# Banded attention and feed-forward on one core: exclusive or in the weight words, a range check by a second read, g folded into w1, seven products from chunk 3, and a new order

## The chip, the cores and the metric

One core of a Trainium2 chip runs the whole program. TensorE (PE; PEld is its weight load), VectorE (DVE), ScalarE (ACT) and GpSimd (POOL) each take their instructions in order; SyncE (SP) issues nearly all DMAs, also in order. The metric is the device time of one execution in microseconds, the median of the runs.

## The reference

```python
scores = scale * np.matmul(q, k.transpose(0, 1, 3, 2))          # (4, 8, 768, 64) each
keep = is_global | is_local                                     # 8 first keys, and the 96 before
scores = np.where(keep, scores + bias, -1e9)
a = np.exp(scores - scores.max(-1)); a = a / (a.sum(-1) + 1e-9)
x = (a @ v) as (4, 768, 512)
xn = (x - mu) / np.sqrt(var + 1e-06) * g_ln
out = x + np.maximum(xn @ w_ch1, 0.0) @ w_ch2                   # (512, 2048) and (2048, 512)
```

[...]

## The kernel before, in words

**Tiles.** The 3072 tokens are 24 tiles of 128 (`t`), two to a chunk (`c`, 12 of them). Tiles 0 to 3 are the first tiles of the four batches; they are "short", with one key block, and are computed in 32-bit floats. All others take two key blocks, with every operand as a high and a low half-precision part, so that a product becomes three.

**Tasks.** All work is given as tasks to a planner (`Plan`), with an engine (or several, with a cost each), a cost, the tasks that it waits for, a rank, and the buffers that it takes. `Plan.order` is a list scheduler on these numbers; what it puts out is the order in which the instructions are written, and each engine then keeps that order. Where PE would idle in the first 90 us it writes products of no use (`blank`). Every instruction is issued through one helper, so all rows have that one line (L204 before, L248 after), and are told apart by their tiles.

**Attention of tile t.** Loads `Lk`, `Lq`, `Lv`; in short tiles `tk`, `tq` (a transpose on PE) and `km`, `qm` (the copy out). `S` scores on PE (tile `s`), `R` mask and row minimum on DVE (`T<-s,mask`), `E` exponentials on ACT, `tp` the transpose of the weights (in long tiles `ph`, `pl` split them and `pt` is a DMA transpose), `P` weights by values (`pv`). Then the normalisation: `X`, `B`, `A` on DVE (`x<-pv,r`, `st<-x`, `mv<-st`), `W` a power on POOL (`rs<-rs,half`), `C` centring on DVE (`xs`), then `xh` and `xl`, the halves of the transposed x (`xT`; for short tiles through a PE transpose `tx`). A long tile with i > 1 also needs 16 key and value rows copied into its neighbour's tile (`gk`, `gv`).

**Weight piece n of 16** (0 to 7 of w1, 8 to 15 of w2): `wb` loads 1 MB, `wr` (ACT) rounds the low word down to three bits, `ws` (DVE) puts the sign into the low word, `wz` (ACT) takes the size of the high word and accumulates a maximum for the range check, `ww` (DVE, `st<-st`, int32) shifts and joins the words, `wu` makes the high half and `wl` the low half.

**Feed-forward.** `F{c}_{f}` is a first-layer step (24 products of 128x256); it needs both tiles' `xT` and weight pieces f//4*2 and the next one. In chunks 0 to 3 (`EVEN = 4`) `hh` and `hl` split its result and `G` is the plain second layer, 96 products of 128x512 a chunk. From chunk 4 on the second layer is done by a seven-product scheme on halves: `hr`, `hm` and `hh`, `hl` make seven mixed operands (`R`, `uh`, `ul`), `N{c}_{n}` are the products (21 of 128x256 for each pair of f, 168 a chunk), `D` combines the sums, and `ya`, `yh`, `yl` make the mixed weights beforehand. `O` stores a tile.

**The end.** `M` (ACT) sums squares of the weights, `K0` judges ranges, `K1` is a small product (`pf`) after `F11_14` that sums over partitions, `K2` writes a flag and `K3` reads it on every engine; it chooses whether a general fallback runs behind.

Of the kernel before, what the change touches and what calls it, by code (L numbers as in the profile page):

```python
# [54 lines left out]
SIDE = (-1.1, 1.1)  # L55
# [24 lines left out]
EVEN = 4  # L80
EARLY = 150.0
LEAD = 11
VRANK = 6.0
VLATE = 0.0
WEIGH = (-0.8, 0.2)
FAVOR = {"ACT": SIDE[0], "POOL": SIDE[1]}
LATER = {"ACT": WEIGH[0], "POOL": WEIGH[1]}
EITHER = {"ACT": 0.62, "DVE": 0.7}
BLANK = 0.22


class Plan:

    def __init__(self, lag=0.12):
        self.tasks, self.room, self.lag, self.blank, self.until = {}, {}, lag, None, 0.0

    def task(self, key, engine, cost, fn, after=(), rank=0.0, take=None, dma=0.0, slack=0.0, port=False):
        assert key not in self.tasks, key
        costs = dict(engine) if isinstance(engine, dict) else {engine: cost}
        self.tasks[key] = costs, fn, [a for a in after if a is not None], rank, take or {}, dma, slack, isinstance(engine, dict), port  # L100

    def order(self):
# [25 lines left out]
        while len(self.times) < len(tasks):  # L128
# [38 lines left out]
            end = t + cost  # L167
# [22 lines left out]
def banded(ctx, tc, q, k, v, n_global, n_local, g_ln, w1, w2, out, flag):  # L190
# [58 lines left out]
    fill = const.tile([P, 1], F32, name="fill")  # L249
# [3 lines left out]
    def starts():  # L253
# [23 lines left out]
    def asked():  # L277
        made["asked"] = counts(const, act, n_global, n_local)
# [49 lines left out]
    task("gb", "SP", 0.6, lambda: load.dma_start(out=gb, in_=g_ln.partition_broadcast(P)), rank=9, dma=0.7)
# [7 lines left out]
    def weight(n):  # L336
# [20 lines left out]
        def signs():  # L357
            vec.tensor_scalar(out=halves[n][:, :, 1], in0=halves[n][:, :, 3], scalar1=0x8000, scalar2=None, op0=ALU.bitwise_and)

        def sizes():  # L360
            hi = staged[n][1]
            act.activation(out=hi.bitcast(F32), in_=hi.bitcast(F32), func=AF.Abs, scale=2.0 ** -111, accum_out=big[:, n:n + 1])

        def whole():
            lo, hi, _, _ = staged[n]
            vec.scalar_tensor_tensor(out=hi, in0=hi, scalar=3, in1=lo, op0=ALU.logical_shift_left, op1=ALU.bitwise_or)

        def upper(engine):
# [12 lines left out]
        task(f"wb{n}", "SP", 0.6, bring, before, rank=rank - 12, take={} if n in homes else {"st": [f"wl{n}"]}, dma=3.0)  # L381
        task(f"wr{n}", "ACT", 1.24, below, [f"wb{n}", "starts"], rank=rank)
        task(f"ws{n}", "DVE", 0.7, signs, [f"wr{n}"], rank=rank, port=True)
        task(f"wz{n}", "ACT", 1.2, sizes, [f"ws{n}"], rank=rank)
        task(f"ww{n}", "DVE", 1.22, whole, [f"wz{n}"], rank=rank, port=True)
        task(f"wu{n}", {"ACT": 1.17, "POOL": 1.95, "DVE": 0.75}, 0, upper, [f"ww{n}"] + (["wl1"] if n == 8 else []) + (["wl3"] if n in (8, 9, 10, 11) else []) + (["wl7", "wl8"] if n >= 12 else []), rank=rank, port=True)
        task(f"wl{n}", {"POOL": 2.2, "DVE": 1.24}, 0, lower, [f"wu{n}"], rank=rank, port=True)
# [16 lines left out]
    def sums_of_weights(j):  # L404
# [26 lines left out]
        cost = {"DVE": 0.68, "POOL": 1.2}  # L431
        last = ["room"] + [f"wl{8 + 2 * j + a}" for a in range(2)]

        def chain_of(n, first, ats, rank, final, last):
# [4 lines left out]
            task(f"yh{n}_{j}", {"ACT": 0.6, "DVE": 0.45}, 0, lambda engine: high(engine, n), last, rank=rank, take={"h": ["never"]} if n == 4 else {}, port=True)  # L439
# [4 lines left out]
        last = chain_of(3, (0, 1), (((0, 1, 1), ALU.subtract), ((1, 0, 1), ALU.add), ((1, 1, 1), ALU.subtract)), rank, 4, last)  # L444
# [3 lines left out]
        chain_of(1, (0, 1), (((0, 0, 0), ALU.subtract), ((1, 0, 1), ALU.add), ((1, 0, 0), ALU.subtract)), rank, 1, last + [f"G{CT * EVEN - CT}_{4 * j + 2}"])  # L448
# [38 lines left out]
    def quick(t, rank):  # L487
# [8 lines left out]
        def loads(name, src, r):  # L496
            task(f"L{name}{t}", "SP", 0.57, lambda: fetch(raw, (name, t), src, name, b, i), rank=rank + r - 12 * (t == 0), take={"ld": [f"P{t}_1" if name == "v" else f"t{name}{t}"]}, dma=1.47)
# [5 lines left out]
        def both(name, make, scale):  # L503
# [8 lines left out]
            task(f"t{name}{t}", "PE", 0.7, flip, [f"L{name}{t}", "ident"], rank=rank, take={bank: [f"{name}m{t}"]}, slack=0.5 * (t > 1))  # L512
# [7 lines left out]
    def keys(t, b, i, rank):  # L520
# [21 lines left out]
        task(f"kh{name}", {"ACT": 0.64, "DVE": 0.5}, 0, high, [f"Lk{name}"], rank=rank, take={"ld": [f"kt{name}"]}, port=True)  # L542
        task(f"kl{name}", {"POOL": 1.22, "DVE": 0.7}, 0, low, [f"kh{name}"], rank=rank, port=True)
# [833 lines left out]
```

## Time and profile before

| what | value |
|---|---|
| time, median of 3 runs | 608.65 us (607.88 to 608.71) |
| profiled execution, first to last instruction | 605.5 us |
| PE, DVE, ACT, POOL busy | 591.0, 514.9, 408.6, 160.8 us |
| granted PE clock over the span | 0.999 |
| DMA moved | 88.33 MB |

The profiled execution shows its span only; the median of the runs is 3.15 us above it, which is what lies before the first and after the last instruction, and the two are compared with that constant between them. Busy shares are averages over a start, in which PE waits for inputs, a long middle, and a tail of a few microseconds.

### The profile page before, as it was taken

Reading aid. Unit: us, or ns where it says so; the run is one execution under the profiler, and the core shown is the slowest. Engines: PE = TensorE matmul, PEld = TensorE weight load, DVE = VectorE, ACT = ScalarE, POOL = GpSimd, SP = SyncE. Lnnn points to the kernel's source line nnn. Section 1 sums busy time; section 2 is a strip of 40 time slices with the busy share of each in tenths; the row PEclk is TensorE's granted clock in tenths of the full one; section 3 lists DMA queues with packets and bytes.
Section 4 is the critical chain, followed back from the end, with each engine's and each line's share of the span. In section 5 each row is a group of like instructions: output and inputs, shape, how many; then the busy total and the mean of one; then the engine's idle time right before and its main releaser. Section 6 shows DMA issues by size and latency. Waiting matters only on the chain.

```text
span 605.5 us, 15320 instructions
## 1 busy us (share of the span) xinstructions
PE 591.0 (98%) x5929; PEld 489.7 (81%) x5929; DVE 514.9 (85%) x1244; ACT 408.6 (67%) x1004; POOL 160.8 (27%) x128
## 2 busy tenths in 40 slices
PE   8989999999999999999999999999999999999996
PEld 4767896556965985789999999999999999988885
DVE  5999999999999989899789999898898788484654
ACT  5988897965677865787765766889856756333330
POOL 2310121306463228242042122152232031040100
PEclk9999999999999999999999999999999999999999
DMA  8993999976879985977748676868865423110001
GB/s 217 321 312 102 238 221 193 244 183 132 221 165 183 183 191 130 202 158 108 156 125 141 139 157 123 162 137 160 154 141 123 105 55 88 36 40 16 35 2 37
DMA packets 247307, 88.33 MB, mean 146 GB/s; under 512 B 237376, under 2 KB 237376, under 8 KB 247232
## 3 DMA queue, kind: packets, MB, share of 16 engines
q1 hardware_dynamic: 246944, 87.32, 65.6%
q8 instruction: 47, 0.77, 0.6%
q14 instruction: 28, 0.23, 0.1%
q10 hardware_dynamic: 288, 0.00, 0.0%
HBM read 38.01 MB, written 6.29 MB: 73 GB/s over the span
## 4 chain that ended last, share of the span: by engine, by line
PE 62%; DVE 5%; DMA 1%; issue 1%; ACT 0%; DVEq 0%
PE f L204 31%; PE m L204 24%; PE s L204 4%; PE pv L204 3%; DMA out_dram<-x 1%; DVE vn L204 1%; DVE T L204 1%; DVE pn L204 1%; DVE x L204 1%; DMA xT<-xn 0%; DVE w2l L204 0%; DVE R L204 0%; DVE xs L204 0%; DVE qn L204 0%; DVE xn L204 0%
## 5 line engine op out<-in xcount | busy, mean ns | idle before, releaser
L204 PE MATMUL f<-xT,w1h 128*128 128x256 f16 x1536 | 256.3, 273 | 4.7 <-DVE xT L204 2.1
L204 PE MATMUL f<-xT,w1l 128*128 128x256 f16 x768 | 209.3, 273 | 0.0
L204 PEld LDWEIGHTS <-w1h 128*128 128x128 f16 x1536 | 147.5, 98 | 21.9 <-DVE xT L204 2.2
L204 DVE SCALAR_TENSOR_TENSOR R<-f,R 128x128 f32<-128x128 f32 x256 | 68.3, 288 | 35.0 <-ACT R L204 29.6
L204 PEld LDWEIGHTS <-uh 128*128 128x128 f16 x896 | 85.9, 98 | 9.4
L204 PEld LDWEIGHTS <-w1l 128*128 128x128 f16 x768 | 75.1, 98 | 9.2 <-issue 0.5
L204 ACT ACTIVATE T<-T,mn 128x256 f32<-128x256 f32 x160 | 80.1, 501 | 3.2
L204 PE MATMUL f<-w2h,h 128*128 128x512 f16 x256 | 80.4, 379 | 0.4 <-DVE h L204 0.4
L204 ACT ACTIVATE uh<-R 128x896 f16<-128x896 f32 x57 | 54.0, 948 | 38.2 <-DVE R L204 37.9
L204 DVE CUSTOM_DVE_ANT_0 T<-s,mask 128x256 f32<-128x256 f32 (+1 forms) x192 | 68.1, 396 | 10.8 <-PE s L204 10.7
L204 ACT ACTIVATE R<-f 128x512 f32<-128x512 f32 x59 | 35.1, 594 | 61.8 <-PE f L204 60.3
L204 PE MATMUL m<-w2h,uh 128*128 128x256 f16 x256 | 69.8, 273 | 0.0
L204 PE MATMUL m<-w2l,uh 128*128 128x256 f16 x256 | 69.8, 273 | 0.0
L204 PE MATMUL m<-w2h,ul 128*128 128x256 f16 x256 | 69.8, 273 | 0.0
L204 PE MATMUL m<-t,uh 128*128 128x256 f16 x384 | 69.5, 273 | 0.0
L204 PEld LDWEIGHTS <-h 128*128 128x128 f16 x384 | 36.3, 98 | 40.0 <-issue 0.6
L204 POOL TENSOR_TENSOR ul<-R,uh 128x896 f16<-128x896 f32 x17 | 32.4, 1907 | 121.4 <-ACT uh L204 121.4
L204 DVE TENSOR_TENSOR ul<-R,uh 128x896 f16<-128x896 f32 x47 | 54.1, 1151 | 12.1 <-ACT uh L204 11.8
L204 POOL TENSOR_TENSOR pn<-T,pn 128x512 f16<-128x512 f32 x27 | 33.8, 1250 | 114.0 <-ACT pn L204 90.1
L204 PE MATMUL s<-kT,qT 128*128 128x128 f16 (+1 forms) x704 | 55.7, 225 | 2.0 <-ACT T L204 0.9
L204 PE MATMUL m<-t,ul 128*128 128x256 f16 x192 | 52.3, 273 | 0.0
L204 ACT ACTIVATE pn<-T 128x512 f16<-128x512 f32 x78 | 48.7, 624 | 2.2 <-DMA xT<-xn 1.1
(155 smaller groups left out, 1018.3 us busy)
## 6 DMA issues: line engine op xcount, KB each, us to landing
st<-in_moe_w_ch_dram SPq DMA_DIRECT2D x10, 1024.0 KB, 6.8
kf<-in_k_dram SPq DMA_DIRECT2D x28, 256.0 KB, 3.9
vf<-in_v_dram SPq DMA_DIRECT2D x28, 256.0 KB, 3.4
qf<-in_q_dram SPq DMA_DIRECT2D x24, 256.0 KB, 3.2
out_dram<-x SPq DMA_DIRECT2D x24, 256.0 KB, 2.4
qT<-qT SPq DMA_DIRECT2D x40, 128.0 KB, 2.7
w2h<-in_moe_w_ch_dram SPq DMA_DIRECT2D x3, 1024.0 KB, 7.3
w2l<-in_moe_w_ch_dram SPq DMA_DIRECT2D x3, 1024.0 KB, 8.3
```

Of the source, the lines that this page charges most:

```text
L204: ins = getattr(self.engine, name)(*args, **kw)
```

## The change

Weights: the words are joined by an exclusive or in place of the or, and the factor that this leaves (`WORD`) is applied when the halves are made; for w1 it is first multiplied by g (`gw`), so that the centred x no longer is. `wz` is gone. The signs may now be taken by ACT, the low halves by DVE alone. The range check reads both matrices again, 64 loads of 256 KB (`V`), each followed by one DVE instruction (`J`), and `JJ` joins the result to the flag. Normalisation: `C` now applies the root as well, so it waits for `W`. The 16 value rows (`gv`) are copied by a DMA instead of by DVE. The seven-product scheme begins at chunk 3 (`EVEN = 3`); its `hm` takes three instructions instead of four. In the last chunk the sums lie otherwise in the banks, and the last tile is stored in two halves. The planner has new costs, margins, a rank for each kind of task (`KINDS`) and for some tasks (`SHIFT`), and fixed engines for some (`GIVEN`).

```diff
-EVEN = 4
-LEAD = 11
+EVEN = 3
+LEAD = 4
...
+MARGIN = {"ACT": 0.1039, "DVE": 0.0395, "POOL": -0.0748}
...
+        rank += KINDS.get(kind(key), 0.0) + SHIFT.get(key, 0.0)
...
-        def sizes():
-            hi = staged[n][1]
-            act.activation(out=hi.bitcast(F32), in_=hi.bitcast(F32), func=AF.Abs, scale=2.0 ** -111, accum_out=big[:, n:n + 1])
...
-            vec.scalar_tensor_tensor(out=hi, in0=hi, scalar=3, in1=lo, op0=ALU.logical_shift_left, op1=ALU.bitwise_or)
+            vec.scalar_tensor_tensor(out=hi, in0=hi, scalar=3, in1=lo, op0=ALU.logical_shift_left, op1=ALU.bitwise_xor)
...
+            if n < NF // 2:
+                for a in range(2):
+                    k0 = 2 * (n % 2) + a
+                    vec.scalar_tensor_tensor(out=dl[:, a], in0=word[:, a], scalar=gw[:, k0:k0 + 1], in1=dh[:, a], op0=ALU.mult, op1=ALU.subtract)
...
-        task(f"ws{n}", "DVE", 0.7, signs, [f"wr{n}"], rank=rank, port=True)
-        task(f"wz{n}", "ACT", 1.2, sizes, [f"ws{n}"], rank=rank)
+        task(f"ws{n}", {"DVE": 1.12, "ACT": 1.13}, 0, signs, [f"wr{n}"], rank=rank, port=True)
...
-            vec.scalar_tensor_tensor(out=xc, in0=xs[t].rearrange("p h d -> p (h d)"), scalar=mv[:, t, 0:1], in1=gb, op0=ALU.subtract, op1=ALU.mult)
+            vec.tensor_scalar(out=xc, in0=xs[t].rearrange("p h d -> p (h d)"), scalar1=mv[:, t, 0:1], scalar2=made["rs", t], op0=ALU.subtract, op1=ALU.mult)
...
+    def read_again(n, tag):
+        st = again[n] = p2.tile([P, 256], I64, tag=tag, name=f"again{n}", bufs=p2_bufs[tag])
...
+            vec.scalar_tensor_tensor(out=made["seen"], in0=hi, scalar=0x30000000, in1=made["seen"], op0=ALU.bitwise_xor, op1=ALU.bitwise_or)
...
+        task(f"V{n_}", "SP", 0.6, lambda n_=n_, tag=tag: read_again(n_, tag), [f"S{B * NT - 1}_1"], rank=1e4 + n_, take={tag: [f"J{n_}"]}, dma=0.8)
...
+    task("JJ", "DVE", 1.2, judge_words, ["K0", f"J{4 * NF - 1}"], rank=1e4)
+    task("K1", "PE", 0.1, across_rows, ["JJ", f"F{NC - 1}_{NF - 2}"], rank=-1e3, take={"s": ["K2"]})
```

On PE, before, the first first-layer step stands between the two weight transposes of tile 2 (`tp2_0`, `tp2_1`); tile 3 comes between the steps behind it.

```order
L204 MATMUL tx1_456<-aside_118,xs1_404 128x128 x4
...
L204 MATMUL tp2_0_478<-ident_89,T2_0_431 128x128 x4
L204 MATMUL tk3_492<-ident_89,kf0_0_401 128x128 x4
...
L204 MATMUL f1_0_0_499<-xT0_334,w1h_83 128x256
...
L204 MATMUL tp2_1_534<-ident_89,T2_1_463 128x128 x4
L204 MATMUL pv2_539<-vf1_0_326,pT2_0_524 128x64 x4
L204 MATMUL tq3_547<-ident_89,qf0_0_429 128x128 x4
```

After, at the same place, only half of tile 3's `pv` and the two `tx` of tiles 2 and 3 are left behind the first step; the eight steps of chunk 0 then have four `blank` products among them.

```order
L248 MATMUL tx1_522<-ident_89,xs1_512 128x128 x4
...
L248 MATMUL pv2_535<-vf1_0_426,pT2_1_527 128x64 x4
...
L248 MATMUL tp3_0_560<-ident_89,T3_0_515 128x128 x4
...
L248 MATMUL tp3_1_582<-ident_89,T3_1_529 128x128 x4
L248 MATMUL pv3_591<-vf0_0_271,pT3_0_569 128x64 x4
...
L248 MATMUL f1_0_0_598<-xT0_327,w1h_83 128x256
```

On DVE, behind the sums of tile 0's x, before: two sign instructions stand ahead of tile 1's chain, a third behind it (`w2h` and `w2l` are where pieces 1 to 3 are staged).

```order
L204 TENSOR_SCALAR w2h_85<-w2h_85 128x1024
L204 TENSOR_SCALAR w2l_86<-w2l_86 128x1024
L204 RECIPROCAL r_305<-r_305 128x8
L204 TENSOR_TENSOR x1_368<-pv1_349,r_305 128x512
L204 BN_STATS st_381<-x1_368 128x6
...
L204 SCALAR_TENSOR_TENSOR w2h_85<-w2h_85 128x1024
L204 TENSOR_SCALAR w2l_86<-w2l_86 128x1024
```

After, at the same place, the signs are gone and the low half of piece 0 and the joining of piece 1 stand there; all high halves that they wait for, of pieces 0 to 4, are on POOL.

```order
L248 SCALAR_TENSOR_TENSOR w1l_84<-w2h_85,gw_91,w1h_83 128x512 x2
L248 TENSOR_SCALAR xs0_373<-x0_328,mv_95,rs_338 128x512
L248 SCALAR_TENSOR_TENSOR w2h_85<-w2h_85 128x1024
L248 RECIPROCAL r_317<-r_317 128x8
L248 TENSOR_TENSOR x1_399<-pv1_353,r_317 128x512
L248 TENSOR_TENSOR xT0_327<-tx0_384,xT0_327 128x4x128
```

On DVE in the last chunk, after: the last of the 64 instructions on the words and the four of `JJ` stand ahead of the mixes of the last first-layer step, F11_14.

```order
L248 SCALAR_TENSOR_TENSOR seen_8440<-again63_9365,seen_8440 128x256
L248 TENSOR_SCALAR seen_8440<-seen_8440 128x256
L248 TENSOR_REDUCE most_9455<-seen_8440 128x1
L248 TENSOR_SCALAR ok_8794<-most_9455 128x1
L248 TENSOR_REDUCE mask0_87<-ok_8794 128x1
L248 SCALAR_TENSOR_TENSOR R_1465<-f1_11_14_9397,R_1465 128x2x128
```

The verdict's `pf` on PE, which was directly behind F11_14, now stands 30 products further on. The loads `V` begin on SP behind tile 23's second scores, which stand between F10_0 and F10_2 on PE.

## Rows read from the trace of the kernel before

**Rows 1.** The page: what the DMA moved in each of 40 slices of the span.
```profile
GB/s 217 321 312 102 238 221 193 244 183 132 221 165 183 183 191 130 202 158 108 156 125 141 139 157 123 162 137 160 154 141 123 105 55 88 36 40 16 35 2 37
```

**Rows 2.** Windows: length, busy us (x instructions) PE, PEld, DVE, ACT, POOL; clock, DMA share, GB/s.
```profile
15.00:30.00 15.00, 13.92 (x102) 10.51 (x103) 13.62 (x37) 14.26 (x39) 4.78 (x3) 1.00 0.94 318
30.00:45.00 15.00, 12.12 (x95) 9.60 (x95) 15.00 (x31) 12.56 (x34) 2.51 (x2) 1.00 0.95 316
45.00:60.00 15.00, 14.02 (x122) 12.10 (x121) 14.21 (x33) 12.89 (x33) 0.92 (x1) 1.00 0.30 95
60.00:75.00 15.00, 14.62 (x128) 12.41 (x128) 14.14 (x22) 13.64 (x22) 2.95 (x2) 1.00 1.12 242
100.00:150.00 50.00, 50.00 (x398) 28.35 (x397) 48.54 (x92) 34.77 (x82) 16.73 (x13) 1.00 0.85 187
500.00:590.00 90.00, 90.00 (x891) 80.81 (x889) 56.94 (x155) 34.51 (x62) 11.37 (x8) 1.00 0.14 36
```

**Rows 3.** Timeline of PE: start, length in us; F0_0, F1_0, the last product.
```profile
38.63 0.28 PE L204 MATMUL f<-xT,w1h 128*128 128x256 f16 x1 [1.78 <-DVE xT L204]
...
43.01 0.61 PE L204 MATMUL tq<-ident,qf 128*128 128x128 f32 x4
43.45 1.00 PE L204 MATMUL pv<-vf,pT 128*128 128x64 f32 x8
44.29 0.38 PE L204 MATMUL f<-xT,w1h 128*128 128x256 f16 x2
...
73.42 0.38 PE L204 MATMUL f<-xT,w1h 128*128 128x256 f16 x2
...
600.39 0.27 PE L204 MATMUL m<-w2h,ul 128*128 128x256 f16 x1
```

**Rows 4.** Timeline of PE in the middle: the starts of successive groups.
```profile
194.88 0.38 PE L204 MATMUL f<-w2l,h 128*128 128x512 f16 x1
195.09 0.38 PE L204 MATMUL f<-w2h,h 128*128 128x512 f16 x1
...
302.93 0.38 PE L204 MATMUL f<-xT,w1h 128*128 128x256 f16 x2
...
308.17 0.27 PE L204 MATMUL m<-w2h,uh 128*128 128x256 f16 x1
...
313.08 0.51 PE L204 MATMUL pv<-vn,pT 128*128 128x64 f16 x12
313.43 0.61 PE L204 MATMUL s<-kT,qT 128*128 128x128 f16 x8
313.88 0.27 PE L204 MATMUL m<-w2h,uh 128*128 128x256 f16 x1
```

**Rows 5.** Timeline of DVE in the start: sign, chain of x, joining, low half.
```profile
21.68 0.19 DVE L204 RECIPROCAL r<-r 128x8 f32<-128x8 f32 x1
...
23.73 1.34 DVE L204 TENSOR_SCALAR w2h<-w2h 128x1024 uint16<-128x1024 uint16 x1
24.86 1.37 DVE L204 TENSOR_SCALAR w2l<-w2l 128x1024 uint16<-128x1024 uint16 x1
...
33.62 1.23 DVE L204 SCALAR_TENSOR_TENSOR w2l<-w2l 128x1024 int32<-128x1024 int32 x1
34.76 0.29 DVE L204 CUSTOM_DVE_ANT_0 T<-s,mask 128x128 f32<-128x128 f32 x1
```

**Rows 6.** Timeline of POOL and DVE where they meet.
```profile
34.98 1.91 POOL L204 TENSOR_TENSOR w1h<-w2l,fill 128x1024 f16<-128x1024 f32 x1 [4.38 <-issue]
35.60 2.37 DVE L204 SCALAR_TENSOR_TENSOR w2l<-w2l 128x1024 int32<-128x1024 int32 x1
```

**Rows 7.** Timeline of DVE in the tail.
```profile
596.53 0.42 DVE L204 SCALAR_TENSOR_TENSOR x<-m,x 128x256 f32<-128x256 f32 x1 [2.68 <-ACT m L204]
596.87 0.41 DVE L204 TENSOR_TENSOR m<-m,m 128x256 f32<-128x256 f32 x1
...
600.70 0.76 DVE L204 SCALAR_TENSOR_TENSOR x<-m,x 128x256 f32<-128x256 f32 x2 [0.54 <-PE m L204]
```

More of the change, by code (lines that the diff above doesn't have):

```diff
@@ L387, in weight @@
-        task(f"wl{n}", {"POOL": 2.2, "DVE": 1.24}, 0, lower, [f"wu{n}"], rank=rank, port=True)
+        task(f"wb{n}", "SP", 0.6, bring, before, rank=rank - 12, slack=0.9, take={} if n in homes else {"st": [f"wl{n}"]}, dma=3.0)
+        first = n < NF // 2
+        task(f"wr{n}", "ACT", 1.12, below, [f"wb{n}", "starts"], rank=rank)
+        task(f"ws{n}", {"DVE": 1.12, "ACT": 1.13}, 0, signs, [f"wr{n}"], rank=rank, port=True)
+        task(f"ww{n}", "DVE", 1.14, whole, [f"ws{n}"], rank=rank, port=True)
@@ L389, in banded @@
+        task(f"wu{n}", {"ACT": 1.29 if first else 1.05, "POOL": 1.95, "DVE": 0.8 if first else 0.62}, 0, upper, [f"ww{n}", "gw"] + (["wl1"] if n == 8 else []) + (["wl3"] if n in (8, 9, 10, 11) else []) + (["wl7", "wl8"] if n >= 12 else []), rank=rank, port=True)
+        task(f"wl{n}", "DVE", 1.32 if first else 1.14, lower, [f"wu{n}"], rank=rank, port=True)
     for n in range(NF):
@@ L438, in chain_of @@
                 last = [key]
-            task(f"yh{n}_{j}", {"ACT": 0.6, "DVE": 0.45}, 0, lambda engine: high(engine, n), last, rank=rank, take={"h": ["never"]} if n == 4 else {}, port=True)
+            task(f"yh{n}_{j}", {"ACT": 0.53, "DVE": 0.34}, 0, lambda engine: high(engine, n), last, rank=rank, take={"h": ["never"]} if n == 4 else {}, port=True)
             task(f"yl{n}_{j}", cost, 0, lambda engine: low(engine, n), [f"yh{n}_{j}"], rank=rank, port=True)
@@ L797, in normal @@
         if not short:
-            task(f"Z{t}", "ACT", 0.2, divisor, [f"E{t}_3"], rank=rank - 4, take={"r": [f"X{t}"]})
-        task(f"X{t}", "DVE", 1.1 if short else 0.92, divide, [last] + ([] if short else [f"Z{t}"]), rank=rank - 4, take={"h" if t == 2 * CT + 1 else "x": [f"O{t}"]})
-        task(f"B{t}", "DVE", 0.72, stats, [f"X{t}"], rank=rank - 4)
-        task(f"A{t}", "DVE", 0.3, spread, [f"B{t}"], rank=rank - 4)
-        task(f"W{t}", "POOL", 0.98, root, [f"A{t}"], rank=rank - 12)
-        task(f"C{t}", "DVE", 0.74, centred, [f"A{t}", "gb"], rank=rank - 4, take={"T": [f"xt{t}" if short else f"xl{t}"]}, port=True)
+            task(f"Z{t}", "ACT", 0.12, divisor, [f"E{t}_{g}" for g in range(4)], rank=rank - 4, take={"r": [f"X{t}"]})
@@ L804, in normal @@
+        task(f"X{t}", "DVE", 0.92, divide, [last] + ([] if short else [f"Z{t}"]), rank=rank - 4, take={"h" if t == 2 * CT + 1 else "x": [f"O{t}"]})
+        task(f"B{t}", "DVE", 0.61, stats, [f"X{t}"], rank=rank - 4)
+        task(f"A{t}", "DVE", 0.29, spread, [f"B{t}"], rank=rank - 4)
+        task(f"W{t}", "POOL", 0.9, root, [f"A{t}"], rank=rank - 12)
+        task(f"C{t}", "DVE", 0.45, centred, [f"W{t}"], rank=rank - 4, take={"T": [f"xt{t}" if short else f"xl{t}"]}, port=True)
         whole = {"xT": [f"F{c}_{NF - 2}"]} if n_ == 0 else {}
@@ L805, in normal @@
         if short:
[L806 to L812 removed]
+            task(f"xt{t}", "PE", 0.44, flip, [f"C{t}"], rank=rank - 20, take={"f1" if t < 2 else "f2": [f"xl{t}"]}, slack=1.0 * (t > 1))
@@ L813, in normal @@
+            task(f"xh{t}", "ACT", 0.49, turned_high, [f"xt{t}"], rank=rank - 4, take=whole)
+            task(f"xl{t}", "DVE", 0.61, turned_low, [f"xh{t}"], rank=rank - 4)
+        else:
+            task(f"xh{t}", "ACT", 0.53, high, [f"C{t}"], rank=rank - 4, take={"pn": [f"xa{t}"]})
+            task(f"xl{t}", "DVE", 0.61, low, [f"xh{t}"], rank=rank - 4, port=True)
             task(f"xa{t}", "SP", 1.35, across, [f"xl{t}"], rank=rank - 12, take=whole, dma=1.47)
@@ L894, in ffn1 @@
         task(key, "PE", 2.62, products, after, rank=rank, take={tag: [f"hl{c}_{f}"]})
-        task(f"hh{c}_{f}", {"ACT": 0.62, "DVE": 0.72}, 0, high, [key], rank=rank - 6, take={"h": last[c:c + 1] if c < 2 else last})
-        task(f"hl{c}_{f}", "DVE", 0.7, low, [f"hh{c}_{f}"], rank=rank - 6)
+        task(f"hh{c}_{f}", {"ACT": 0.49, "DVE": 0.61}, 0, high, [key], rank=rank - 6, take={"h": last[c:c + 1] if c < 2 else last})
+        task(f"hl{c}_{f}", "DVE", 0.6, low, [f"hh{c}_{f}"], rank=rank - 6)
         steps.append(key)
@@ L942, in banded, with where @@
     UAT = {1: 0, 2: 1, 7: 2, 4: 3, 5: 4, 6: 5, 3: 6}
+    def where(c, m):
+        return (3, 1) if m == 3 and c == NC - 1 else WHERE[m]
     def factor(m, j, a):
@@ L1076, in banded @@
         tile_(t, [QUICK[t]] * 2, [[], []])
-    for c in range(NC):
+    for c in range(EVEN):
         if c < 2:
@@ L1100, in banded @@
     for t in range(2 * CT, B * NT):
-        when = [8 + 2 * (4 * (t - 2 * CT) + g) - (LEAD if t >= CT * EVEN else 0) for g in range(4)]
+        when = [8 + 2 * (4 * (t - 2 * CT) + g) - (LEAD if t >= max(CT * EVEN, 6) else 0) for g in range(4)]
         tile_(t, [due(w) for w in when], [[steps[w - 1]] for w in when])
```

277 lines of the change are left out of this document (158 added, 119 removed), and 19 rows, old and new, of tables (GIVEN, KINDS, SHIFT).

## The prediction

> **What bounds the kernel now.** I read the page first, then the windows, then PE's timeline from its first useful product to its last. By the page PE is busy for 98% of the span. A matmul's end is modelled, so what PE really takes is read from starts [rows 4]: 48 first-layer products of 256 columns stand between 302.93 and 308.17, which is 0.109 us each; a product of 512 columns takes 0.21 to 0.22, twice that; a group of twelve `pv` 0.35, a group of eight scores 0.45. F1_0 starts at 73.42 and the last product at 600.39 [rows 3]. Between them lie 11 chunks of 192 first-layer products (231 us), four plain second layers of 96 (84 us), eight of seven products with 168 each (147 us), and 80 groups each of scores and `pv` (63 us). That is 525 of the 527 us. From F1_0 on PE works at its pace with 2 us of gaps, and nothing but fewer products, or a new wait, can move that part.
>
> The 73 us before are another stage. In the four windows from 15 to 75 us DVE is busy for 57 of 60 us and PE does filling products [rows 2]. F0_0 waits for DVE's `xT` [rows 3], and the eight steps of chunk 0 then take 34.8 us, where 8 x 24 x 0.109 = 21.0 would do. So DVE's ordered list sets the start, and the DMA, at 316 to 318 GB/s from 15 to 45 us [rows 2], is close behind it.
>
> **Start, the ledger of DVE.** Prices: a sign 1.13 us (start to start), a joining of words 1.14, four masked sums 0.84, the chain X, B, A of a tile 2.05 [rows 5, 6]. Up to the low half of tile 3's x, before F1_0, the old order has ten signs and the new one has one: -10.2. Low halves go from seven to eight and come in two parts with the factor, which I put at 1.25 for the 1.14 of a joining of the same length: +2.0. One joining more: +1.1. The others (three splits of q, k or v, two high halves and eight masks fewer, shorter centring; three copies and one relu more) are each half as long as a joining or shorter and come to about -2. Sum: 9 us less DVE work ahead of F1_0.
>
> **Start, the first product.** It does begin later. Ahead of tile 1's `xT`, the new order has three signs fewer (-3.4), a joining more (+1.1), four low halves for two (+2.7), tile 2's chain (+2.0), tile 3's eight masked sums (+1.7), three copies of some 0.6 more (+1.8), and masks, a high half and centring less (-2.7): +3.2, so F0_0 begins near 41.8. But little is then left: 21.0 us of products, half a `pv` (0.84 for eight products), two `tx` of four (0.44 each, as a `tq`) and four fillers (0.22 each) are 23.6 us [rows 3, 4]. F1_0 then starts at 65.4, and the 9 us of the ledger give 64.4. What ACT gets in place of the signs it can take: `wz`, which falls away there, is an instruction over the same 1024 words. The first two weight pieces now stand behind six and seven loads of 256 KB; at 317 GB/s a load is 0.83 us and a piece 3.3, so both are some 13 us of transfer, ahead of their turn on DVE.
>
> **Start, POOL against DVE.** The rows show what speaks against this order. While POOL made a high half for 1.91 us, a joining on DVE that began 0.62 us later took 2.37 us in place of 1.23 [rows 5, 6]; it ended one joining after POOL did. The new order puts five high halves (pieces 0 to 4) and five masks on POOL. Each meeting costs DVE up to 1.15 us by this row. Bounds: 0 if the planner's order keeps them apart, as it intends, and 5 x 1.15 = 5.8. I take 2, two meetings, since behind the joinings of pieces 3 and 4 DVE has two-input instructions next. So F1_0 starts at 67.5, 5.9 us earlier than before.
>
> The Trainium skill's page "SBUF — State Buffer", in "Who interferes with whom", says that DVE and GpSimd share a port pair by an exclusive lock, which a DVE instruction with two SBUF inputs needs against a GpSimd instruction that reads SBUF; the loser waits for the whole instruction. By this rule five meetings from their starts cost 5 x 1.91 = 9.6 us; the row agrees with the kind of wait and shows 1.15 of it. Taken in full it is the second rival below.
>
> **Middle.** Chunk 3 needs 168 products of 0.109 (18.4 us) in place of 96 of 0.219 (21.0): -2.6 us, on PE's own path. Its operands cost DVE more (`hm`, `hl`), and the mixed weights are needed a chunk earlier; this lies under PE, since DVE gives up the 16 copies of value rows, shorter mixes and the sign instructions. From 100 to 150 us DVE is already at 48.5 of 50 [rows 2], and it begins this stretch 6 us earlier with nearly the same work per product, so the cover is thin: if it fails, `hl` is late and PE waits. The 16 value copies by DMA have 5.4 us or more of PE work between the tile's last `pv` and the next tile's first; I put them at nothing.
>
> **End.** The re-read is 64 x 262144 B = 16.8 MB. It begins behind tile 23's second scores, and `pf` waits for it. Between them PE has 360 first-layer and 324 second-layer products at 0.109, six groups of `pv` and three of scores: 78 us. At 317 GB/s the loads take 53 us, at the 187 GB/s of 100 to 150 us they take 90 [rows 2]. The DMA is nearly idle there now, 0.14 from 500 to 590 us, so I take the upper rate: it fits. DVE is idle for 33 of these 90 us. 64 instructions at 0.34 (start to start) to 0.41 (a whole instruction of that size) [rows 7] are 22 to 26 us, and about seven eighths of a tile's attention moves into this stretch (`LEAD` is 7 steps less), some 9 us by the two chains, sums and splits of a tile. 31 to 35 against 33: just full, and in order, with each `J` waiting for its load. I allow 2 us of new PE gaps for middle and end together, from 0 to the rival's price. The tail gains 0.4: the last two steps on DVE take 0.76 [rows 7], and one of them now goes ahead of the last product.
>
> **Sum.** -5.9 - 2.6 - 0.4 + 2.0 = -6.9 us. The execution of 605.5 us becomes 598.6, and with the 3.15 us around it, the 608.65 of the runs becomes 601.7.
>
> **Rivals.**
> *Clean start.* No meeting costs anything and no new gap appears: F1_0 at 65.4, so -8.0 - 2.6 - 0.4 = -11, 597.6. For it: the planner knows the shared use. Against it: DVE and PE are then both full from 42 to 75 us.
> *The lock in full.* 9.6 us on DVE's list put F1_0 at 75.0, +1.6: with the rest +0.6, 609.2, no gain. Against it: the one meeting in the rows cost 1.15, and masked sums run through POOL's instruction undisturbed [rows 6].
> *The re-read is late* (the other side). At 187 GB/s it ends 90 us after it began, 12 to 15 us after `pf` is due; PE stands there, since the product waits in order, and the time is 601.7 + 15 = 617. It decides from the point where the lateness exceeds 7 us, that is, 81 us less 4 for the last joins: below some 205 to 215 GB/s. For it: only 1 of 40 slices from the second third on reaches 200 GB/s [rows 1], though nothing asked for it. Against it: rows of 2 KB, and an empty queue.
>
> **Numbers.** Forecast (599 to 605) 0.57; clean start 0.16; lock in full 0.09; late re-read 0.13, of which a third is a lateness of a few us that still leaves a gain; anything else 0.05. The range reaches from 596 (beyond the clean start) to 608, which leaves out most of the late re-read and half of the lock. A change of 0.2% (1.2 us) is about what a measurement of this kernel can tell from none. Faster by more than that 0.82, within it 0.06, slower 0.12.
>
> **What the profile after would show.** First product at 41 to 44 us and F1_0 at 65 to 70, with DVE full between; two-input DVE instructions that last beyond 2 us beside POOL's high halves, at most three; no PE wait over 1 us between 100 and 500 us; 168 `m` products more and 128x512 `f` products down to three quarters; 64 loads that keep over 220 GB/s until the last chunk, and a `pf` that follows its neighbour without a gap. Wrong would be: F0_0 after 48 us; PE waits in front of `pv` or `m` of a microsecond each; a wait at `pf`.

## The result: slower by 1.4%

| what | before | forecast | after |
|---|---|---|---|
| time, median | 608.6 us (607.9 to 608.7) | 601.7 (596 to 608) | 616.7 us (615.6 to 617.0) |
| ratio, 95% interval | | 0.989 | 1.0136 (1.0112 to 1.016) |
| profiled span, us | 605.5 | 598.6 | 614.8 |
| F0_0 starts | 38.63 | 41.8 | 52.27 |
| F1_0 starts | 73.42 | 67.5 | 78.52 |
| F1_0 to last product | 526.97 | 526.4 | 531.07 |
| last product to end | 5.1 | 4.7 | 5.2 |

The change is slower, by about 8 us, and outside the range. F0_0 and F1_0 are the first products of chunks 0 and 1. F1_0 is 5.1 us later instead of 5.9 earlier, a miss of 11.0, and the stretch behind it 4.1 us longer instead of 0.6 shorter.

Profile after, the page's slices: the granted clock in tenths, and GB/s. Slices 35 to 39, from 522 us on, now carry the second read.

```profile
PEclk9998999999999899999999999999999999999999
GB/s 177 341 236 176 218 225 273 139 181 181 189 160 146 133 103 108 139 154 131 174 194 137 115 158 122 181 164 96 182 157 90 156 120 102 230 253 209 370 199 38
```

Windows after, columns as in [rows 2]. From 15 to 75 us it is ACT that is full (14.9, 14.9, 13.3, 15.0 of 15), and DVE, full before, is not (12.9 to 13.6); it waits for ACT. The clock is below 1 from 30 to 60 us.

```profile
15.00:30.00 15.00, 14.05 (x113) 11.37 (x112) 12.85 (x45) 14.90 (x44) 7.45 (x8) 1.00 1.13 337
30.00:45.00 15.00, 12.38 (x72) 7.61 (x70) 13.60 (x46) 14.87 (x28) 6.28 (x4) 0.95 0.71 261
45.00:60.00 15.00, 15.00 (x108) 12.61 (x108) 13.07 (x21) 13.28 (x25) 2.88 (x2) 0.82 0.47 144
60.00:75.00 15.00, 12.62 (x111) 10.55 (x109) 12.92 (x20) 15.00 (x18) 1.93 (x2) 1.00 1.07 243
100.00:150.00 50.00, 49.17 (x392) 26.77 (x390) 47.81 (x102) 37.38 (x86) 16.29 (x13) 1.00 0.97 174
500.00:590.00 90.00, 90.00 (x938) 81.36 (x936) 78.68 (x205) 42.35 (x90) 10.02 (x8) 1.00 0.77 220
```

PE's timeline after: the first load, the gap in the start, F0_0, F1_0, the waits of the middle, the verdict, the last product.

```profile
8.41 1.11 PE L248 MATMUL tk<-ident,kf 128*128 128x128 f32 x4 [3.66 <-DMA kf<-in_k_dram]
...
42.91 0.66 PE L248 MATMUL tx<-ident,xs 128*128 128x128 f32 x4 [2.19 <-DVE xs L248]
...
52.27 0.38 PE L248 MATMUL f<-xT,w1h 128*128 128x256 f16 x2
...
78.52 0.27 PE L248 MATMUL f<-xT,w1h 128*128 128x256 f16 x1
...
103.45 0.39 PE L248 MATMUL f<-w2h,h 128*128 128x512 f16 x1 [0.83 <-DVE h L248]
...
168.28 0.39 PE L248 MATMUL f<-xT,w1h 128*128 128x256 f16 x2 [1.34 <-DVE h L248]
...
208.73 0.62 PE L248 MATMUL s<-kT,qT 128*128 128x128 f16 x8 [0.53 <-DVE nm L248]
211.35 0.80 PE L248 MATMUL pv<-vn,pT 128*128 128x64 f16 x12 [2.00 <-DVE x L248]
...
601.35 0.21 PE L248 MATMUL pf<-mask,ones 128*1 128x27 f32 x2 [0.40 <-DVE mask L248]
...
609.59 0.27 PE L248 MATMUL m<-w2h,ul 128*128 128x256 f16 x1
```

Three things stand in the start that the forecast did not have. The first, ACT's timeline after: a sign (`w2h<-w2h`) lasts 2.5 us, 2.25 until the next instruction starts. A weight comes as a 64-bit word, which the program takes as two of 32 bits; the sign instruction reads the high one and writes 16 bits of the low one, so that its results lie 8 bytes apart.

```profile
25.75 2.52 ACT L248 ACTIVATE w2h<-w2h 128x1024 f16<-128x1024 f32 x1
28.00 0.69 ACT L248 ACTIVATE kT<-tk 128x512 f32<-128x512 f32 x1
...
30.64 2.52 ACT L248 ACTIVATE w2l<-w2l 128x1024 f16<-128x1024 f32 x1
```

ACT's and DVE's timelines before: the `wz` by which I priced it, and the first masked sum.

```profile
25.37 1.15 ACT L204 ACTIVATE w2h<-w2h 128x1024 f32<-128x1024 f32 x1
...
10.01 0.29 DVE L204 CUSTOM_DVE_ANT_0 T<-s,mask 128x128 f32<-128x128 f32 x1 [0.98 <-PE s L204]
```

DVE's timeline after: joinings wait for ACT's sign, and a pair of low halves takes 3.06 us.

```profile
28.30 1.23 DVE L248 SCALAR_TENSOR_TENSOR w2h<-w2h 128x1024 int32<-128x1024 int32 x1 [1.30 <-ACT w2h L248]
...
38.20 1.23 DVE L248 SCALAR_TENSOR_TENSOR w2l<-w2l 128x1024 int32<-128x1024 int32 x1 [1.33 <-ACT w2l L248]
39.34 3.06 DVE L248 SCALAR_TENSOR_TENSOR w1l<-w2l,gw,w1h 128x512 f16<-128x512 f32 x2
```

POOL's timeline after, the high half beside that pair:

```profile
39.50 2.35 POOL L248 TENSOR_TENSOR w1h<-w2l,gw 128x1024 f16<-128x1024 f32 x1 [2.60 <-DVE w2l L248]
```

The second thing is the first key load: PE has it at 8.41 us, before at 4.65 (PE's timeline before), so DVE's first sum is at 14.14 instead of 10.01.

```profile
4.65 1.11 PE L204 MATMUL tk<-ident,kf 128*128 128x128 f32 x4
```

The third is the clock: windows after, columns as above.

```profile
40.00:44.00 4.00, 1.75 (x10) 1.15 (x10) 4.00 (x14) 3.94 (x6) 1.85 (x1) 0.93 0.07 28
44.00:48.00 4.00, 4.00 (x19) 3.63 (x19) 4.00 (x9) 3.71 (x19) 2.24 (x1) 0.50 0.00 0
48.00:52.00 4.00, 4.00 (x22) 2.65 (x21) 3.79 (x9) 2.60 (x4) 0.64 (x2) 0.71 0.50 163
```

PE stands for 2.2 us up to 42.91; then the granted clock is 0.50, the 1.2 GHz level, until about 50 us.

### The profile page after: what moved, and what is told of

The parts are those of the page before. It is cut to its first block, busy times and chain, and to the rows that moved or that the text cites. A ratio compares the mean times of both kernels' runs of the same rounds, so it can differ in the third digit from the quotient of the medians.

```text
span 614.8 us, 15630 instructions
## 1 busy us (share of the span) xinstructions
PE 593.2 (96%) x5983; PEld 498.9 (81%) x5983; DVE 525.6 (85%) x1277; ACT 419.3 (68%) x990; POOL 125.0 (20%) x108
## 4 chain that ended last, share of the span: by engine, by line
PE 58%; DVE 11%; issue 2%; ACT 1%; DMA 1%; DVEq 0%; ACTq 0%
PE f L248 27%; PE m L248 23%; PE s L248 4%; PE pv L248 3%; DVE seen L248 3%; DVE R L248 1%; DVE x L248 1%; DVE h L248 1%; DVE va L248 1%; DVE T L248 1%; DMA again<-in_moe_w_ch_dram 1%; DVE pn L248 1%; DVE ul L248 0%; DVE t L248 0%; ACT T L248 0%
## 5 line engine op out<-in xcount | busy, mean ns | idle before, releaser
L248 PEld LDWEIGHTS <-uh 128*128 128x128 f16 x1008 | 95.8, 98 | 10.3
L248 ACT ACTIVATE uh<-R 128x896 f16<-128x896 f32 x71 | 66.9, 944 | 46.0 <-DVE R L248 45.8
L248 PE MATMUL m<-w2h,uh 128*128 128x256 f16 x288 | 78.5, 273 | 0.0
L248 PE MATMUL m<-w2l,uh 128*128 128x256 f16 x288 | 78.5, 273 | 0.0
L248 PE MATMUL m<-w2h,ul 128*128 128x256 f16 x288 | 78.5, 273 | 0.0
L248 PE MATMUL m<-t,uh 128*128 128x256 f16 x432 | 78.3, 273 | 0.0
L248 DVE SCALAR_TENSOR_TENSOR R<-f,R 128x128 f32<-128x128 f32 (+1 forms) x216 | 71.8, 334 | 7.5 <-ACT R L248 2.3
L248 DVE TENSOR_TENSOR ul<-R,uh 128x896 f16<-128x896 f32 x60 | 67.1, 1122 | 6.3 <-ACT uh L248 6.0
L248 PE MATMUL f<-w2h,h 128*128 128x512 f16 x192 | 60.1, 379 | 0.8 <-DVE h L248 0.8
L248 DVE TENSOR_TENSOR pn<-T,pn 128x512 f16<-128x512 f32 x63 | 49.2, 784 | 13.0 <-ACT pn L248 12.6
L248 PEld LDWEIGHTS <-ul 128*128 128x128 f16 x504 | 49.3, 98 | 5.8
L248 PEld LDWEIGHTS <-h 128*128 128x128 f16 x288 | 27.0, 98 | 31.1 <-DVE h L248 1.3
L248 PEld LDWEIGHTS <-qT 128*128 128x128 f16 x640 | 42.0, 98 | 5.6 <-DVE nm L248 0.8
```

The source lines that it names most:

```text
L248: ins = getattr(self.engine, name)(*args, **kw)
```

## The experiments

Ratios are to the kernel before, of the same chip and batch; 0.001 is 0.6 us. The change itself is 1.0136.

**e1: the price of ACT's sign.**

```diff
-act.activation(out=halves[n][:, :, 1].bitcast(F16), in_=staged[n][1].bitcast(F32), func=AF.Copy, scale=2.0 ** -60)
+act.activation(out=staged[n][1].bitcast(F32), in_=staged[n][1].bitcast(F32), func=AF.Copy, scale=1.0)
```

> The changed kernel in its own order, but the 14 sign instructions on ACT are replaced by a copy of the high word onto itself, in the form that the old wz had (1024 words, 32-bit in and out); so the sign never reaches the low word, and the output's values are of other weights. In the trace of the changed kernel a sign on ACT lasts 2.5 us (2.25 from start to start), where wz took 1.15. Theory A (the signs on ACT are twice as dear as I took them, and the start waits for them): four stand ahead of F0_0, so F0_0 comes 4 to 4.5 us earlier than 52.3, near 48, F1_0 as much earlier than 78.2, and the time falls from 616.7 to about 612. Rival (DVE's list sets the start anyway, ACT has room): DVE loses only its two waits of 1.3 us for ACT or nothing at all, and the time stays above 614.

Ratio 0.999 (0.9965 to 1.0015): 8.9 us less than the change, twice what I expected. F0_0 starts at 47.75. The timelines of ACT, DVE and PE show the price, the wait that is gone, and F1_0:

```profile
25.76 1.17 ACT L248 ACTIVATE w2h<-w2h 128x1024 f32<-128x1024 f32 x1
```

```profile
26.96 1.23 DVE L248 SCALAR_TENSOR_TENSOR w2h<-w2h 128x1024 int32<-128x1024 int32 x1
```

```profile
72.30 0.38 PE L248 MATMUL f<-xT,w1h 128*128 128x256 f16 x2
```

From F1_0 to the last product it takes 528.0 instead of 531.1: the waits for `h` at 103 and 168 fall to 0.2 or less each. So the price costs some 6 us ahead of F1_0 and 3 behind. The copy takes 1.03 us from start to start, a little less than the 1.14 of a `wz` with its accumulation.

**e2: PE kept busy over the gap** ahead of tile 1's `tx` (task `xt1`).

```diff
+MORE = {"xt1": 9}
...
+            order += [(t, len(order), self.blank)] * MORE.get(key, 0)
```

> The changed kernel in its own order with nine more products of no use ahead of tile 1's tx, which fill the 2.19 us in which PE stands at 40.7 to 42.9 us. In the trace of the changed kernel the granted clock is 0.50 from 43.3 to 50.1 us, behind that gap. Theory B (the gap costs the clock, and the clock costs the start): the clock stays at 1.00, two pv groups and two transposes of weights take half as long, ACT's wait of 1.61 us for tp goes, and F0_0 comes 1.4 us earlier: 615.3. Rival (DVE and ACT hold the path through this stretch): the clock is 1.00, but F0_0 and the time stay within 0.3 us.

Ratio 1.0109 (1.0084 to 1.0135). The window shows the clock kept:

```profile
44.00:48.00 4.00, 4.00 (x31) 3.10 (x30) 4.00 (x13) 3.97 (x19) 1.92 (x1) 1.00 0.00 0
```

F0_0 is 1.4 us earlier (50.90) and F1_0 about 1.1, in this one profile. The medians differ by 1.6 us with overlapping intervals: the clock's part is about a microsecond, and no more can be said.

**e3: `EVEN = 4` in the changed kernel.**

```diff
-EVEN = 3
+EVEN = 4
```

> The changed kernel with the seven-product scheme beginning at chunk 4 again (EVEN = 4), everything else as changed; the planner orders anew behind the first chunks. In the trace of the changed kernel PE loses 6.2 us between 80 and 220 us (0.99 at 102, 1.5 at 167, 3.5 at 208 to 211, and 2.9 at the lower clock behind that), and before it lost next to nothing there and 1.4 at 256. Theory C (the earlier mixes and mixed weights overload DVE, which is full there): the stalls at 208 to 217 go, 6 us are won, 2.6 are lost on chunk 3's products: 613. Rival (the stalls come from the late start or from the tables of ranks, not from chunk 3): the stalls stay or move, and only the loss of 2.6 is seen: 619.

Ratio 1.0285 (1.0255 to 1.0314), worse than either theory. In place of the stall at 208 us stands one of 1.3 us at 206, and others stand elsewhere, in PE's timeline:

```profile
154.61 0.61 PE L248 MATMUL s<-kT,qT 128*128 128x128 f16 x8 [3.00 <-DVE kT L248]
...
430.76 0.52 PE L248 MATMUL pv<-vn,pT 128*128 128x64 f16 x12 [1.85 <-DMA pT<-pn]
433.58 0.82 PE L248 MATMUL pv<-vn,pT 128*128 128x64 f16 x12 [2.30 <-DMA pT<-pn]
```

The planner orders everything behind anew, with tables made for 3. Theory C falls as stated; the run does not measure the 2.6 us of chunk 3.

**e4: all 14 signs of ACT on DVE**, at the same place in the order.

```diff
+OVER = {f"ws{n}": "DVE" for n in range(16)}
...
+            engine = OVER.get(key, engine)
             order.append((t, len(order), (lambda fn=fn, engine=engine: fn(engine)) if told else fn))
```

> The changed kernel in its own order, but all 14 sign instructions of ACT go to DVE, at the same place in the order; the signs are right. DVE gets five signs of 1.13 us more ahead of F0_0, ACT is rid of five times 2.25. Theory A in its strong form (ACT is the bound of the start now): F0_0 comes earlier by about what ACT is rid of beyond its own waits, 3 to 5 us: 612 to 614. Rival (DVE's list is the bound, as I predicted): F0_0 comes 5 us later, and DVE between 75 and 200 us gets nine signs more, which it can't hide: 622 or more.

Ratio 1.0227 (1.0199 to 1.0255), 622.0 us: the rival. Its windows show DVE full and ACT with room:

```profile
30.00:45.00 15.00, 11.20 (x55) 7.23 (x54) 14.93 (x30) 6.37 (x21) 5.26 (x4) 0.79 0.73 268
45.00:60.00 15.00, 13.07 (x107) 11.18 (x106) 14.79 (x35) 9.36 (x25) 2.90 (x2) 0.99 0.39 140
60.00:75.00 15.00, 11.98 (x104) 9.83 (x102) 14.83 (x23) 9.17 (x13) 2.14 (x2) 1.00 0.95 235
```

So DVE has no room for the signs either: five of them ahead of F0_0 cost as much as ACT's price saves.

**e5: the sign read as 16 bits.**

```diff
-act.activation(..., in_=staged[n][1].bitcast(F32), ...)
+act.activation(..., in_=halves[n][:, :, 3].bitcast(BF16), ...)
```

> The changed kernel in its own order; a sign on ACT reads the upper 16 bits of the high word in place of its 32 bits, and writes the same 16 bits as before, with the right sign. With the copy in 32-bit form (e1) an instruction of the same length took 1.15 us in place of 2.25 and the time fell by 8.3 us. Theory A1 (reading 32 bits and writing 16 with a step of 8 bytes is what is slow): the sign takes about 1.15, and the time is that of e1, about 608. Theory A2 (writing 16 bits with a step of 8 bytes is slow by itself): it stays at 2.25 and the time at 615 to 616.

Ratio 1.0118 (1.0098 to 1.0137). ACT's timeline: 16 bits in, the same length. It is not the reading, so A2. That it is the 16-bit width at this step is the likely cause, but not parted from the rest: the copy of e1 also writes the other word and has another factor (1 in place of 2**-60). The 8.3 us of the expectation are 8.9 by the ratios.

```profile
25.11 2.52 ACT L248 ACTIVATE w2h<-w2h 128x1024 f16<-128x1024 bf16 x1
```

**e6: the first loads as before.**

```diff
-        (act, sp)[n].dma_start(out=made["asked"][:, n, :], in_=src.bitcast(I32).partition_broadcast(P))
+        (act, act)[n].dma_start(out=made["asked"][:, n, :], in_=src.bitcast(I32).partition_broadcast(P))
...
-            task(..., lambda: fetch(raw, (name, t), src, name, b, i, act if aside else None), ...)
+            task(..., lambda: fetch(raw, (name, t), src, name, b, i), ...)
```

> The changed kernel in its own order, but both counts are asked for on ACT's queue and tile 0's q is loaded on SP behind its k, as before the change; one issue moves to each queue and nothing else. In the trace of the changed kernel the first transpose waits for the first k until 8.41 us, in the trace of before it starts at 4.65, and DVE's first masked sums begin at 14.14 and 10.01. Theory D (the first loads are 4 us of the late start): k lands near 4.7, the first sums begin near 10, and F0_0 and the time come 3 to 4 us earlier, 612 to 613. Rival (the weight pieces and ACT's list hold the start, so the early attention is only done sooner): sums near 10, but F0_0 and the time less than 1.5 us earlier.

Ratio 1.0066 (1.0047 to 1.0085), 4.3 us less: theory D. PE's first transpose, then DVE's first sum:

```profile
4.78 1.11 PE L248 MATMUL tk<-ident,kf 128*128 128x128 f32 x4
```

```profile
9.86 0.29 DVE L248 CUSTOM_DVE_ANT_0 T<-s,mask 128x128 f32<-128x128 f32 x1 [1.03 <-ACT mask L248]
```

PE's timeline, F1_0, 3.9 us earlier:

```profile
74.67 0.27 PE L248 MATMUL f<-xT,w1h 128*128 128x256 f16 x1
```

The two edits, the count ahead of k on SP and tile 0's q beside it on the other queue, were not run apart. The traces part them a little: from 2 to 4 us the DMA moved 2 GB/s in the change, when each queue had a count ahead of its first large load, and 123 in e6 (122 before). So some 1.5 us of the 3.8 are a stand of both loads; in the rest k and q were under way together.

**e7: `EVEN = 3` in the kernel before.**

```diff
-EVEN = 4
+EVEN = 3
```

> The kernel before with one number changed: the seven-product scheme begins at chunk 3 (EVEN = 3). By the ledger chunk 3 needs 2.6 us less of PE. Theory C1 (the scheme pays wherever PE is the bound, and e3 lost 10 us because the other tables were made for EVEN = 3): 605 to 606.5. Rival C2 (an earlier start of the scheme overloads DVE, which is full from 100 to 200 us; the stall that stood at 256 comes at about 210 and is longer): 608 or more.

Ratio 1.03 (1.0281 to 1.0319): 18 us slower. Waits of PE add up at several places: 3.4 us for `xT` at 153, 3.1 for `R` at 221, 5.0 for a transposed `pT` at 262, 2.2 for `R` at 330. By the time it is rival C2. By the waits DVE is one part of it, some 7 us; some 10 are waits for DMA transposes (`xT`, `pT`), and what held those was not followed. The 2.6 us of products are small against what an earlier start of the scheme does to an order that was not made for it.

**e8: no second read**, but for one load and one instruction of the 64.

```diff
-    for n_ in range(4 * NF):
+    for n_ in range(1):
...
-    task("JJ", "DVE", 1.2, judge_words, ["K0", f"J{4 * NF - 1}"], rank=1e4)
+    task("JJ", "DVE", 1.2, judge_words, ["K0", "J0"], rank=1e4)
```

> The changed kernel with one of the 64 loads of the second read and one of its 64 instructions on DVE; the range check of the other words is left out. The time of this shows what the second read costs in the end. My step (it fits: only pf's wait of 0.4 us in the trace and the joins behind it are left): 0 to 0.8 us faster, 615 to 616. Rival (its loads and DVE instructions also push back the attention of the last tiles and the stores): 2 us or more faster.

Ratio 1.011 (1.009 to 1.0129). 1.6 us less, with overlapping intervals. Its profiled span is 3.3 us shorter than that of the change, but 1.7 of it stand ahead of F1_0 already, and 1.2 around 208 us, where the clock fell less; both are ahead of all that was left out. So the second read costs about 0.5 us by this one profile, as the step has it.

**e9: e1 and e6 together.**

> The changed kernel in its own order with the edits of e1 (sign instructions of ACT in the 32-bit form at 1.15 us; the signs are left out) and of e6 (first loads as before) together. Against the kernel before, e1 was at 0.999 and e6 at 1.0066, the change itself at 1.0136, which is 8.8 and 4.2 us. If both stand one behind the other on the path of the start, they add up: 616 - 13 = 603, F0_0 near 43.7 and F1_0 near 68, and my ledger of the start was right but for these two. If they share one wait, the sum stays above 606.

Ratio 0.993 (0.9906 to 0.9953), 604.6 us: 12.5 us less than the change, and 8.9 + 4.3 = 13.2 are the parts; they add up. PE's timeline, F0_0 and F1_0; from there to the last product it takes 528.1.

```profile
44.23 0.27 PE L248 MATMUL f<-xT,w1h 128*128 128x256 f16 x1
...
69.03 0.27 PE L248 MATMUL f<-xT,w1h 128*128 128x256 f16 x1
```

**e10: e9, and the high halves of pieces 3 and 4 on DVE.**

```diff
+OVER = {"wu3": "DVE", "wu4": "DVE"}
...
+            engine = OVER.get(key, engine)
```

> As e9, and the high halves of pieces 3 and 4 go from POOL to DVE, at the same place in the order. In the traces of the change and of e1 a pair of low halves on DVE beside them takes 3.06 us in place of 1.41, twice. Theory L (POOL's instruction holds the two-input one up): DVE gets two pairs of 0.8 to 0.9 more and is rid of twice 1.65, so both pairs last 1.41, and F0_0 and the time come 1 to 1.6 us earlier than e9. Rival (the long pairs come from something else, such as the length of the operands): the pairs stay at 3 us, and the time is 1.6 us later.

Ratio 0.9916 (0.9892 to 0.9941), about 1 us on e9 with overlapping intervals. DVE's timeline tells it better. The second pair, beside which POOL now does nothing, takes 1.40; the first still stands beside POOL's high half of another piece (34.08, 2.35 us).

```profile
33.91 3.06 DVE L252 SCALAR_TENSOR_TENSOR w1l<-w2l,gw,w1h 128x512 f16<-128x512 f32 x2
...
40.18 1.40 DVE L252 SCALAR_TENSOR_TENSOR w1l<-w2l,gw,w1h 128x512 f16<-128x512 f32 x2
```

A meeting costs 3.06 - 1.40 = 1.66 us. The Trainium skill's page "SBUF — State Buffer", "Who interferes with whom", on which the second rival rested, has the loser wait for the whole instruction; by POOL's length that would be 1.9, an estimate. 1.66 is nearer to it than the 1.15 that I took.

**e11: tile 8's X ahead**, in e6: a step of the mixes (`va`) and `R<-f` go behind it.

```diff
+AHEAD = {"ya12_2": "ya10_3", "hr3_0": "ya10_3"}
...
+        for key, other in AHEAD.items():
+            task = place[key]
+            order.remove(task)
+            order.insert(order.index(place[other]), task)
```

> The kernel of e6, with two DVE instructions moved: where the seven-product scheme begins, one step of the weight mixes (va) and the first relu of chunk 3 (R<-f) go behind tile 8's X in place of ahead of it. In the traces of the change, e1, e6 and e9 alike, PE stands 2.0 us there with a pv that waits for that X, and the granted clock is near 0.5 to 0.6 for some 4 us behind it. Theory M (DVE's order at this place is what stalls, not the sum of its work): pv comes 1.8 us earlier, the clock keeps up better, and the time falls 1.5 to 3 us below e6 (612.3), to about 610. Rival (DVE is behind by its whole list): the wait moves to the next f, which needs R, and the time stays.

Ratio 1.0056 (1.0036 to 1.0076), not told from e6. PE's timeline shows the wait moved, as the rival has it: `pv` waits 0.29 instead of 2.0, and the next `f` 1.80 for `R`.

```profile
205.16 0.62 PE L257 MATMUL s<-kT,qT 128*128 128x128 f16 x8 [0.53 <-DVE nm L257]
206.07 0.51 PE L257 MATMUL pv<-vn,pT 128*128 128x64 f16 x12 [0.29 <-DVE x L257]
...
208.38 0.38 PE L257 MATMUL f<-xT,w1h 128*128 128x256 f16 x2 [1.80 <-DVE R L257]
```

DVE is behind as a whole where the scheme begins, not at one instruction.

**e12: a version out of what the runs showed**, on e11.

```diff
+OVER = {**{f"ws{n}": "DVE" for n in (1, 2, 5, 7, 9, 10, 12, 13)}, "wu3": "DVE", "wu4": "DVE"}
+MORE = {"xt1": 5}
```

> A version with all outputs right, out of what the runs showed: the change, with the first loads of e6, the order of e11, five of the products of no use of e2, the high halves of pieces 3 and 4 on DVE as in e10, and 8 of the 14 signs of ACT (pieces 1, 2, 5, 7, 9, 10, 12, 13) on DVE, those behind which DVE waited 0.4 to 1.7 us for ACT in the trace of e6. Theory (ACT's sign costs 2.25 where DVE's costs 1.13 of a wait that is there anyway): it gains 3 to 5 us on e11 and reaches 605 to 607, ahead of both kernels. Rival (DVE is as full as in e4, where all 14 signs on DVE gave 622): 612 or more.

Ratio 1.0032 (1.002 to 1.0043), 610.1 us: 6 us better than the change, 2 worse than before. F1_0 starts at 73.1, where the kernel before has it. Half the signs on DVE is a middle way, no way out.

**e13 and e14: the signs on POOL**, in e6; in e14 also the high halves of pieces 1 to 4 on ACT.

```diff
+OVER = {f"ws{n}": "POOL" for n in range(1, 16)}
...
+            if engine == "POOL":
+                pool.tensor_scalar(out=halves[n][:, :, 1].bitcast(F16), in0=staged[n][1].bitcast(F32), scalar1=2.0 ** -60, scalar2=None, op0=ALU.mult)
+                return
```

> The kernel of e6 (first loads as before) in its own order, with all 14 signs of ACT made by POOL, by the same multiplication that ACT used; the signs are right. POOL is busy for 7.5, 6.3 and 2.9 of each 15 us from 15 to 60 in the trace of the change. Theory A (ACT's price): if a sign takes POOL about 1.9 us, as its high halves do, and DVE's two-input instructions are held up for 1 us each by some of them, the start gains most of e9's: F1_0 near 70 and 605 to 608. Rival (POOL's meetings with DVE cost as much as ACT's price): F1_0 at 75 or later and 612 or more.

> As e13, and the high halves of pieces 1 to 4 go from POOL to ACT, in two instructions of some 0.65 us each, so that in the start POOL has about the load of the changed kernel and ACT is rid of 2.25 - 1.3 us for each of these pieces. Theory A: 605 to 607, a little better than e13. Rival (meetings): better than e13 by the meetings of four high halves, 2 to 4 us, but still above 608.

Ratios 1.0485 (1.0456 to 1.0514) and 1.0418 (1.04 to 1.0437). The edit takes a sign of DVE to POOL too, 15 in all. POOL's timeline in e13:

```profile
13.64 1.66 POOL L252 TENSOR_SCALAR mask<-d 128x256 bf16<-128x256 f32 x2
...
22.30 4.28 POOL L252 TENSOR_SCALAR w2h<-w2h 128x1024 f16<-128x1024 f32 x1
...
27.92 1.89 POOL L252 TENSOR_TENSOR w1h<-w2h,gw 128x1024 f16<-128x1024 f32 x1 [1.34 <-DVE w2h L252]
```

The sign takes 4.28 us there, the high half 1.89; DVE waits up to 3.9 for it. My 1.9 was the same mistake as in the forecast, a price taken from an instruction of the same length but of another form. Here the step of the result is not shown to be the reason: the two differ in the operation too, and a mask, of the sign's operation with a dense 16-bit result, takes 0.83 us for 256 elements. If that goes by length, 1024 would take 3.3 (an estimate). Theory A was thus not tried on POOL; all three engines that could take the sign have a price for it that the start pays.

## Why the prediction was wrong, step by step

**What bounds the kernel, and the ledger of DVE.** Right in kind. That DVE is busy for less of each 15 us (12.9 to 13.6, before 13.6 to 15.0 [rows 2]) does not show it, since it waits: 7.7 us between 14.5 and 78.5. e9 does: there DVE stands ready for the last half of tile 3's x at 67.3, where it began it at 72.6 before. Some counts were off: by the traces, up to that half the new order has two joinings more and not one, one split less and not three, two copies more and not three. By the ledger's prices that is some 1.7 us too much gain, and F1_0 at 66.1 by DVE's list; it did not matter much, since by PE's products F1_0 stood at 65.4. But the ledger was kept for one engine, and the work moved onto another.

**"What ACT gets in place of the signs it can take."** This is the step that failed. I priced a sign at `wz`'s length, 1.15, because both go over 1024 words; it takes 2.25, and ACT became the engine that the start waits for. e1 gives this one price: 8.9 us, of which I had none.

**First product.** I looked for the weight pieces behind the moved loads and found them early enough. The very first loads were moved too, and I did not follow them: k0 arrives 3.8 us later, and e6 puts that at 4.3 us. Both terms together (e9) bring F1_0 to 69.0; the forecast was 67.5. Of the 16.2 us by which the profiled span missed (614.8 for 598.6) they take 12.4; the other 3.8 are 1.5 up to F1_0, 1.7 from there to the last product, and 0.6 behind it.

**POOL against DVE.** The mechanism was right, the size not: two meetings with high halves ahead of F1_0, as allowed for, but at 1.66 each, 3.3 us for the 2 taken (a third, of 0.9 us, stands beside another POOL instruction at 67 us). With this correction the sum for F1_0 is 67.5 + 1.3 = 68.8, and e9 has 69.0. So close a fit is in part luck: with 3.3 for the meetings F0_0 should be at 45.1 and is at 44.2, and the stretch from there to F1_0 is 24.8 instead of 23.6. The first rival is thus out, and the second was right only in the price.

**Clock.** Not in the forecast at all, in either half: the new gap of 2.2 us in the start is followed by 7 us at 0.50, and the stall at 208 to 211 by 0.50 again from 212 to 216. e2 puts the first at some 1 us of the time; at the second, e8's profile, with 0.74, 0.83 and 1.00 in the three windows from 208 to 220 where the change has 0.84, 0.50 and 0.81, is 1.2 us shorter there.

**Middle.** Forecast -2.6 for chunk 3 and +2 of new gaps for middle and end; it came to +4.1. Of this 3 go with ACT's price (e1). What is left is +1.1 in e9. There PE waits for 2.8 us where the scheme begins and has a clock of 0.57 from 200 to 204 us, which is 1.7 us of the four; before, it waited for 1.1 us where the scheme began. Against the 2.6 these give +0.8, an estimate that fits; that chunk 3 alone would gain 2.6 was shown by no run. e11 shows that the cover which I called thin fails there: DVE is late as a whole. e7 shows how much the order counts: with the old one the same edit costs 18 us.

**End.** Right. The loads are issued from 520.6 to 592.2 us, DVE is fuller (78.7 of 90, before 56.9), and `pf` waits 0.40 us. The third rival did not come: that its 617 is the time that was measured is chance. The 0.4 us of the tail did not come either: 5.2 us behind the last product, before 5.1.

Of what the profile was to show, three signs that I had named for "wrong" came: F0_0 after 48, a wait of a microsecond or more in front of `pv`, and a (short) one at `pf`.

## What to carry to other kernels

When work moves from a full engine to a second one, price it there by an instruction of the same operation with the same form of result (width and step), not by the length alone, and keep a ledger for that engine as well: ACT was idle for 0.7 to 2.4 us of each 15 [rows 2], and a sign in place of a `wz` takes it 1.1 us more for each piece. Follow the first load of the program as closely as the ones in the diff; everything behind it moves by the same time. One number of a planner (`EVEN`) can't be costed alone when its tables were made for the other value.

## What the runs showed of the hardware that was not expected

On ACT a 16-bit result written with a step of 8 bytes took twice the time of others of its length: 2.52 us, 2.25 from start to start, where a 32-bit result at the same step took 1.17, 1.03 from start to start (e1), and a dense 16-bit one 1.17 as well. Reading 16 or 32 bits made no difference (e5); the factor of the instruction was not varied by itself. On DVE a sign took 1.13 [rows 5]. On POOL it took 4.28, and a dense result of the same operation 0.83 for a quarter of the length, so that there the step need not be the reason.

In a meeting both engines lose: the pair of low halves on DVE takes 1.66 us more (3.06 for 1.40), and POOL's instruction 2.35 instead of 1.90.
